# Second layers two first layers later, gate rounding on GpSimd, and a third tile's copies on VectorE, in a fused attention and MLP kernel

## The chip, the cores and the metric

The kernel runs on one core of a Trainium2 chip. Its engines work side by side, each through its own queue in order: TensorE (PE in the profile; PEld are its weight loads), VectorE (DVE), ScalarE (ACT), GpSimd (POOL) and SyncE (SP, which issues most DMAs). The metric is the device time of one execution in microseconds (us), as a median of several runs.

## The reference

Banded attention (each query sees the last 96 keys and 8 global ones, with a slope per head), and then a two-layer MLP over its output. All in float32.

```python
scores = scale * np.matmul(q, k.transpose(0, 1, 3, 2))      # 4 batches, 8 heads, 768 x 768, head size 64
bias = -slopes[:, None, None] * dist[None, :, :]
scores = np.where(keep, scores + bias[None], -1000000000.0)
a = np.exp(scores - np.max(scores, axis=-1, keepdims=True))
a = a / (np.sum(a, axis=-1, keepdims=True) + 1e-09)
x = np.matmul(a, v)                                          # -> 3072 tokens of 512
...
h = x @ w_in                                                 # 512 -> 2048
g = h * np.clip(h + 3.0, 0.0, 6.0) / 6.0
return (g @ w_out).astype(np.float32)                        # 2048 -> 512
```

## The kernel before

**Tiling.** The 3072 tokens are 8 blocks of 384 (three tiles of 128). A block's attention is done in four pairs of heads. A block's MLP runs over 16 slices of 128 hidden columns. For one slice the *first layer* (`first`, L179) is 12 matmuls into one PSUM bank hp (there are two), the *gate* makes g from hp (ACT relu L190, DVE L191), splits it into a rounded part gh (`high`, L197 on GpSimd or L199 on ACT) and the rest gl (`rest`, DVE L204), and the *second layer* (`second`, L211) is 9 matmuls that add gh and gl times w_out into three PSUM banks acc. Each product uses high and low parts, hence the three matmuls where one would do. g has one buffer, gh and gl three each (`common`, L116 and L117).

**Weights.** They lie in memory as 16 words of 1 MB, two 32-bit halves per number, and are decoded on the chip (`decode`, L403). Even words hold two slices of w_in, odd words the same two slices of w_out, so the first layer of slice f needs word f//2*2 and its second layer word f//2*2+1. A word's decoding takes three steps, written here as a, b and c:

- a: the fetch of the word two later, DVE L417 and L418, ACT L395
- b: DVE L424 of the word before (its low part)
- c: DVE L427 (needs L395 and L418), then for the next word ACT L384 and GpSimd L388, then ACT L431 (the high part)

The scratch `we`, which L388 writes, L395 completes and L427 reads, has one buffer; L388 of the next word therefore follows L427 of this one.

**Stages.** (1) The attention of blocks 0 and 1: eight pairs, each as scores (L862), `weigh` (DVE L877, ACT L881), normalizing (GpSimd L901), `turn` (PE transposes of each of the three tiles, L909 and L911, and the copy pt of them from PSUM, L913), and `values` (L953) with `put_x` (ACT L165 for xh, DVE L166 for xl). In it `self.more` is true until the last scores are out: up to then (pairs 0 to 5) tile 1's copy runs on DVE, those of tiles 0 and 2 on ACT; afterwards all on ACT. (2) The MLP of block 0, with four slices of block 1 among it, while the weights are still being decoded; it begins in the last two pairs' `turn`. (3) The other 12 slices of block 1 beside the attention of block 2 (`beside`, L630). (4) Blocks 2 to 7, each beside the attention of the next.

**What sets the order.** The instructions of PE, SyncE and GpSimd run in the order of the program (`in_order`, L651). Those of DVE and ACT are put in order by the framework's scheduler, at build time. The program order of stage 2 comes from the generator `halves` (L452): for each slice of `order` (L619) it emits the first layer and the gate, then the second layer of the slice before, kept in `self.last`, and yields after each. `work` (L434) keeps two counters, one for PE time and one for DVE time, and emits a decoding step whenever DVE's is behind; `decoded_to` (L447) forces the steps that the next layer needs. `finish` (L488) emits the pending second layer.

`order` puts slices 0 to 3 of block 1 behind slices 4, 7, 10 and 13 of block 0. `halves` is called without `pool` for blocks 0 and 1, so that gh is rounded on ACT (L199), and with it from block 2 on (L197).

Of the kernel before, what the change touches and what calls it, by code (L numbers as in the profile page):

```python
# [26 lines left out]
NF = DF // P  # L27
# [23 lines left out]
BESIDE = 12  # L51
LEAST_AHEAD = 4
WORDS = 2
# [9 lines left out]
class Kernel:  # L63
# [377 lines left out]
    def decode_step(self):  # L441
        self.given[1] += next(self.decoding_steps)
        self.decoded += 1
        if self.decoded == 3 * (NF + 1):
            self.decoded_all()

    def decoded_to(self, i):  # L447

        while self.decoded < 3 * (i + 1) + (2 if i < NF - 1 else 3):
            self.decode_step()  # L450

    def halves(self, steps, pool=False):  # L452


        for block, f, x, acc in steps:
            self.decoded_to(f // 2 * 2)
            g = self.gate(self.first(f, x), block == len(self.blocks) - 1 and f == NF - 1)
            gh = self.high(g, pool) if pool else None
            self.work(2.1, 0.47)
            yield  # L460
            if not pool:
                gh = self.high(g, pool)
            gl = self.rest(g, gh)
            self.work(0, 0.47)
            if self.last is not None:
                self.finish()
                yield
            self.last = (block, f, acc, gh, gl)

# [18 lines left out]
    def finish(self):  # L488
        block, f, acc, gh, gl = self.last
        self.decoded_to(f // 2 * 2 + 1)  # L490
        self.second(f, acc, gh, gl)
        if f == NF - 1 and block < len(self.blocks) - 1:
            b, tb = self.blocks[block]
            self.store(b * S + tb * TB, acc)
        self.ended = block, f
        self.work(2.1, 0)
        self.last = None

    def banded(self, flag):
# [9 lines left out]
        self.raw, self.z, self.e, self.given, self.decoded = {}, {}, {}, [0.0, 0.0], 0  # L509
        self.last, self.op, self.ended = None, None, None  # L510
        self.weights()
        with ExitStack() as early, ExitStack() as words:
# [69 lines left out]
            self.weights()  # L582
            self.allowed = 3 * (NF + 1)
            acc1 += [pool.tile([P, BANK], F32, name=name) for pool, name in ((self.ps_s, "sp"), (self.ps_t, "tp"), (self.ps_x, "xp"))]
# [14 lines left out]
        for i in range(2, len(self.blocks)):  # L599
            units, x_next = [], None  # L600
            if i + 1 < len(self.blocks):
                x_next = self.x_tiles()
                units, ahead = self.attention(i + 1, x_next, ahead)
                if i == 2:
                    units = [[]] + units
            else:
                units = [[]] * 4 + [[lambda: self.doubt(flag)]]
            acc = self.acc_tiles()
            steps = [(i, f, x, acc) for f in range(NF)]
            for k, _ in enumerate(self.halves(steps if x_next else steps[:-3], True)):  # L610
                for unit in units[k] if k < len(units) else ():
                    unit()
            if not x_next:
                self.end(steps[-3:])
            x = x_next
# [3 lines left out]
    def order(self, xs, acc, acc1):  # L619
# [3 lines left out]
        for f in range(NF):  # L623
            steps.append((0, f, xs[0], acc))
            while done * (NF - LEAST_AHEAD) < (f + 1 - LEAST_AHEAD) * (NF - BESIDE):
                steps.append((1, done, xs[1], acc1))
                done += 1
# [171 lines left out]
class Pair:  # L799
# [103 lines left out]
    def turn(self, t):  # L903
# [8 lines left out]
        c = slice(0, 1 if lo else 2)  # L912
        (nc.vector.tensor_copy if kk.more and t == 1 else nc.scalar.copy)(out=pt[:, :, c], in_=tp[:, :, c])  # L913
        self.pts.append(pt)
# [120 lines left out]
```

## Time and profile before

| | us |
|---|---|
| median of 3 runs (lowest to highest) | 677.55 (677.43 to 677.74) |
| the profiled execution | 679.32 |
| its span, first to last instruction | 677.5 |

The profile is of one execution, whose time is 1.8 us over its span. Three views of it are read below: the page (share of each engine), the waits (which engine waited for whom), and windows and timelines (busy time of each engine in a stretch, and its instructions one by one: start in us, duration in us, engine, line, operation, what is written and read, and in brackets the idle time before it and what ended it). A duration on the timeline can overlap the next instruction's, so a queue's pace is read from the starts.

The 40 slices of the page, each 16.9 us long, in tenths of busy time, and the clock that TensorE was granted:

```profile
PE   9878898999998999999999999999999999999997
DVE  6778899524564776557662677547763677422222
ACT  6988899434553444143332444143331433221111
PEclk9969899999999999999999999999999999999999
```

Stages 1 and 2 fill the first nine slices, to about 152 us; stage 3 ends near 214 us.

### The profile page before, as it was taken

The page shows a single profiled execution, that of the slowest core. Times are in us where ns is not written, and L with a number is a line of the kernel's source. Part 1 is how long each engine was busy: PE and PEld are TensorE (multiplying, and loading weights), DVE is VectorE, ACT ScalarE, POOL GpSimd, SP SyncE. Part 2 cuts the span into 40 slices and gives each one's busy share as a digit, 9 for nine tenths or more (in the row PEclk, how much of TensorE's full clock was granted, in tenths as well). Part 3 has the DMA queues.
Part 4 walks back from the last instruction along what each step waited for, and adds up shares of the span by engine and source line. Part 5 has one row for each costly group of instructions (what it writes and reads, how often), then busy time and mean ns, then how long its engine had stood idle before and what let it go on. Part 6 is the DMA issues. An engine that isn't in the chain of part 4 may idle for free.

```text
span 677.5 us, 11187 instructions
## 1 busy us (share of the span) xinstructions
PE 655.5 (97%) x3923; PEld 582.1 (86%) x3923; DVE 406.7 (60%) x1068; ACT 294.3 (43%) x714; POOL 212.3 (31%) x373
## 2 busy tenths in 40 slices
PE   9878898999998999999999999999999999999997
PEld 7667787898787999999998999899998999999995
DVE  6778899524564776557662677547763677422222
ACT  6988899434553444143332444143331433221111
POOL 5744232001221333325340444404541344302110
PEclk9969899999999999999999999999999999999999
DMA  8645655003575357634554257634455155500001
GB/s 321 185 162 180 247 218 186 1 1 97 153 210 156 98 156 194 171 105 125 153 157 126 91 148 194 172 112 117 125 164 156 62 154 150 139 33 18 1 1 51
DMA packets 67169, 89.56 MB, mean 132 GB/s; under 512 B 10656, under 2 KB 53920, under 8 KB 65056
## 3 DMA queue, kind: packets, MB, share of 16 engines
q1 hardware_dynamic: 66816, 88.49, 43.8%
q8 instruction: 33, 0.54, 0.3%
q14 instruction: 32, 0.26, 0.1%
q10 hardware_dynamic: 288, 0.26, 0.1%
HBM read 65.14 MB, written 23.59 MB: 131 GB/s over the span
## 4 chain that ended last, share of the span: by engine, by line
PE 75%; DVE 9%; DMA 5%; issue 4%; ACT 4%; POOL 2%; SPq 0%; POOLq 0%; DVEq 0%; ACTq 0%
PE hp L179 33%; PE acc L211 31%; PE xp L953 3%; PE sp L866 2%; ACT n L881 2%; DMA load<-pairs 2%; DVE wz L427 2%; PE tp L953 2%; PE tp L866 2%; POOL n L901 1%; DVE n L877 1%; DVE wz L417 1%; DMA wst<-w 1%; DVE g L191 1%; DVE gl L204 1%
## 5 line engine op out<-in xcount | busy, mean ns | idle before, releaser
L190 ACT ACTIVATE g<-hp,small 128x384 f32<-128x384 f32 x127 | 73.6, 580 | 246.0 <-PE hp L179 228.5
L179 PE MATMUL hp<-xh,w1h 128*128 128x384 f32 x512 | 174.6, 341 | 0.0
L179 PE MATMUL hp<-xh,w1l 128*128 128x384 f32 x512 | 172.9, 338 | 0.0
L179 PE MATMUL hp<-xl,w1h 128*128 128x384 f32 x512 | 172.5, 337 | 0.0
L197 POOL TENSOR_SCALAR gh<-g 128x384 fp32r<-128x384 f32 x96 | 51.8, 540 | 296.6 <-DVE g L191 257.5
L211 PE MATMUL acc<-w2h,gl 128*128 128x512 f32 x336 | 133.7, 398 | 5.4 <-DVE gl L204 5.4
L901 POOL TENSOR_SCALAR n<-n,sums 128x232 f32<-128x232 f32 (+1 forms) x186 | 99.0, 548 | 108.6 <-ACT n L881 61.1
L211 PE MATMUL acc<-w2h,gh 128*128 128x512 f32 x336 | 132.4, 394 | 0.4 <-ACT gh L199 0.4
L211 PE MATMUL acc<-w2l,gh 128*128 128x512 f32 x336 | 132.3, 394 | 0.0
L191 DVE SCALAR_TENSOR_TENSOR g<-g,hp 128x384 f32<-128x384 f32 x128 | 69.8, 545 | 89.8 <-ACT g L190 89.4
L881 ACT ACTIVATE n<-n,least 128x232 f32<-128x232 f32 (+1 forms) x192 | 89.2, 466 | 50.5 <-DVE least L877 49.8
L204 DVE TENSOR_TENSOR gl<-g,gh 128x384 fp32r<-128x384 f32 x128 | 78.4, 613 | 52.5 <-POOL gh L197 44.9
L179 PEld LDWEIGHTS hp<-xh,w1h 128*128 128x128 f32 x512 | 96.7, 189 | 6.0 <-issue 2.2
L179 PEld LDWEIGHTS hp<-xl,w1h 128*128 128x128 f32 x512 | 96.7, 189 | 3.7
L179 PEld LDWEIGHTS hp<-xh,w1l 128*128 128x128 f32 x512 | 96.5, 188 | 0.0
L211 PEld LDWEIGHTS acc<-w2h,gl 128*128 128x128 f32 x336 | 63.1, 188 | 23.0 <-DVE gl L204 9.5
L926 DVE STREAM_TRANSPOSE blocks<-n 128x256 f32<-128x256 f32 x132 | 51.5, 425 | 36.3 <-POOL n L901 25.4
L211 PEld LDWEIGHTS acc<-w2h,gh 128*128 128x128 f32 x336 | 63.3, 188 | 10.7 <-ACT gh L199 0.7
L211 PEld LDWEIGHTS acc<-w2l,gh 128*128 128x128 f32 x336 | 63.2, 188 | 10.1
L877 DVE CUSTOM_DVE_ANT_0 n<-sp,d 128x232 f32<-128x232 f32 (+1 forms) x70 | 23.7, 376 | 30.8 <-PE sp L866 30.5
L388 POOL TENSOR_SCALAR we<-wst 128x1024 int32<-128x1024 uint32 x16 | 22.7, 1416 | 46.1 <-DVE wz L427 37.5
L881 ACT ACTIVATION_READ_ACCUMULATOR n<-n,least 128x1 f32 x192 | 36.1, 188 | 0.0
(120 smaller groups left out, 745.6 us busy)
## 6 DMA issues: line engine op xcount, KB each, us to landing
wst<-w SPq DMA_DIRECT2D x16, 1024.0 KB, 4.9
there<-blocks SPq DMA_DIRECT2D x60, 256.0 KB, 2.6
load<-pairs SPq DMA_DIRECT2D x20, 636.0 KB, 5.2
load<-pairs SPq DMA_DIRECT2D x32, 384.0 KB, 4.1
weights<-there SPq DMA_DIRECT2D x48, 192.0 KB, 4.0
weights<-there SPq DMA_DIRECT2D x48, 160.0 KB, 3.2
out<-o SPq DMA_DIRECT2D x23, 256.0 KB, 2.0
load<-pairs SPq DMA_DIRECT2D x11, 444.0 KB, 4.4
```

The lines of the kernel that those rows point to most:

```text
L179: self.nc.tensor.matmul(hp, lhsT=self.w1(w, f)[:, kt, :], rhs=a[:, kt, :], start=(n == 0), stop=(n == 3 * NKT - 1))
L190: nc.scalar.activation(out=g, in_=hp, func=AF.Relu, bias=self.three, scale=1.0)
L191: nc.vector.scalar_tensor_tensor(out=g, in0=g, scalar=6.0, in1=hp, op0=ALU.min, op1=ALU.mult)
L197: self.nc.gpsimd.tensor_scalar(out=gh, in0=g, scalar1=1.0, scalar2=0.0, op0=ALU.mult, op1=ALU.add)
L204: self.nc.vector.tensor_tensor(out=gl, in0=g, in1=gh.bitcast(F32), op=ALU.subtract)
L211: self.nc.tensor.matmul(acc[tt], lhsT=a[:, tk], rhs=self.w2(w, f), start=(f == 0 and j == 0), stop=(f == NF - 1 and j == 2))
L866: nc.tensor.matmul(sp[j][:, lo:W], lhsT=q[:, t], rhs=part["kx"][:, c], start=(m == 0), stop=(m == 1))
L877: nc.vector.tensor_tensor_reduce(out=e[:, j, lo:W], in0=sp[j][:, lo:W], in1=d, op0=ALU.add, op1=ALU.min, scale=scale, scalar=3.0e38, accum ...
L881: nc.scalar.activation(out=e[:, j, lo:W], in_=e[:, j, lo:W], func=AF.Exp, bias=self.least[:, i:i + 1], scale=-1.0, accum_out=self.sums[:, ...
L901: nc.gpsimd.tensor_scalar(out=e[:, j, lo:W], in0=e[:, j, lo:W], scalar1=over, scalar2=0.0, op0=ALU.mult, op1=ALU.add)
L926: nc.vector.transpose(out=blocks[:, :, s].rearrange("p b j q -> p j b q"), in_=e[:, :, c:c + P].rearrange("p j (b q) -> p j b q", b=4))
L953: nc.tensor.matmul(xps[j * D:(j + 1) * D, t * P:(t + 1) * P], lhsT=vt[0:K, t, j * D:(j + 1) * D], rhs=self.part(t, j, c, K), start=(c == 0 ...
```

## The change

- While the weights are being decoded, `self.last` is a list of up to two pending second layers: that of a slice is emitted after the first layer of the slice two later in the list. Once all is decoded, it is one again.
- Before a first layer whose word is not yet decoded, the pending second layers are emitted.
- `order` puts the four slices of block 1 behind slices 3, 4, 5 and 6 of block 0.
- gh is rounded on ACT only in slices started before the end of stage 1 (`self.early`, cleared there); the other slices of blocks 0 and 1 use GpSimd.
- While `self.more` holds, DVE copies tile 2's transposes as well as tile 1's.

With the first layer of block b, slice f written Fb.f and the second Sb.f, the program order of PE's halves from the last pairs on, worked out from the two counters, is:

```
before: F0.0 F0.1 S0.0 F0.2 S0.1 F0.3 S0.2 F0.4 S0.3 F1.0 S0.4 F0.5 S1.0 F0.6 S0.5 F0.7 S0.6 F1.1 S0.7 F0.8 S1.1 F0.9 S0.8 F0.10 S0.9 F1.2 S0.10 F0.11 S1.2 F0.12 S0.11 F0.13 S0.12 F1.3 S0.13 F0.14 S1.3 F0.15 S0.14 F1.4 S0.15
after:  F0.0 F0.1 S0.0 S0.1 F0.2 F0.3 F1.0 S0.2 F0.4 S0.3 F1.1 S1.0 F0.5 S0.4 F1.2 S1.1 F0.6 S0.5 F1.3 S1.2 F0.7 S0.6 F0.8 S1.3 F0.9 S0.7 F0.10 S0.8 F0.11 S0.9 F0.12 S0.10 S0.11 F0.13 S0.12 F0.14 S0.13 F0.15 S0.14 F1.4 S0.15
```

```diff
-LEAST_AHEAD = 4
+LAG = 3
...
-        if self.decoded == 3 * (NF + 1):
+        if self.decoded == self.all_steps:
             self.decoded_all()
 
+    def ready(self, i):
+        return self.decoded >= 3 * (i + 1) + (2 if i < NF - 1 else 3)
+
     def decoded_to(self, i):
-        while self.decoded < 3 * (i + 1) + (2 if i < NF - 1 else 3):
+        while not self.ready(i):
             self.decode_step()
 
-    def halves(self, steps, pool=False):
+    def halves(self, steps):
         for block, f, x, acc in steps:
+            while self.last and not self.ready(f // 2 * 2):
+                self.finish()
+                yield
             self.decoded_to(f // 2 * 2)
             g = self.gate(self.first(f, x), block == len(self.blocks) - 1 and f == NF - 1)
+            pool = not self.early
             gh = self.high(g, pool) if pool else None
             self.work(2.1, 0.47)
             yield
...
             gl = self.rest(g, gh)
             self.work(0, 0.47)
-            if self.last is not None:
+            while len(self.last) >= (2 if self.decoded < self.all_steps else 1):
                 self.finish()
                 yield
-            self.last = (block, f, acc, gh, gl)
+            self.last.append((block, f, acc, gh, gl))
...
     def finish(self):
-        block, f, acc, gh, gl = self.last
+        block, f, acc, gh, gl = self.last.pop(0)
...
             self.weights()
-            self.allowed = 3 * (NF + 1)
+            self.early = False
+            self.allowed = self.all_steps
...
             steps.append((0, f, xs[0], acc))
-            while done * (NF - LEAST_AHEAD) < (f + 1 - LEAST_AHEAD) * (NF - BESIDE):
+            if LAG <= f < LAG + NF - BESIDE:
                 steps.append((1, done, xs[1], acc1))
                 done += 1
...
-        (nc.vector.tensor_copy if kk.more and t == 1 else nc.scalar.copy)(out=pt[:, :, c], in_=tp[:, :, c])
+        (nc.vector.tensor_copy if kk.more and t > 0 else nc.scalar.copy)(out=pt[:, :, c], in_=tp[:, :, c])
```

More of the change, by code (lines that the diff above doesn't have):

```diff
@@ L496, in finish @@
         self.work(2.1, 0)
-        self.last = None
     def banded(self, flag):
@@ L509, in banded @@
         self.raw, self.z, self.e, self.given, self.decoded = {}, {}, {}, [0.0, 0.0], 0
-        self.last, self.op, self.ended = None, None, None
+        self.last, self.op, self.ended, self.early, self.all_steps = [], None, None, True, 3 * (NF + 1)
         self.weights()
@@ L609, in banded @@
             steps = [(i, f, x, acc) for f in range(NF)]
-            for k, _ in enumerate(self.halves(steps if x_next else steps[:-3], True)):
+            for k, _ in enumerate(self.halves(steps if x_next else steps[:-3])):
                 for unit in units[k] if k < len(units) else ():
```

## The prediction

> **What bounds the kernel now.** I read the page first, then what TensorE (PE) waits for, then its stretches. A *half* below is one first layer (12 matmuls, L179) or one second layer (9 matmuls, L211) of one slice; F0.3 is the first layer of block 0, slice 3, and S1.0 the second layer of block 1, slice 0.
>
> ```profile
> span 677.5 us, 11187 instructions
> PE 655.5 (97%) x3923; PEld 582.1 (86%) x3923; DVE 406.7 (60%) x1068; ACT 294.3 (43%) x714; POOL 212.3 (31%) x373
> L197 POOL TENSOR_SCALAR gh<-g 128x384 fp32r<-128x384 f32 x96 | 51.8, 540 | 296.6 <-DVE g L191 257.5
> ...
> PE acc L211 <- DVE gl L204: 5.4, 8, 1.9
> PE xp L953 <- issue: 5.2, 2, 3.2
> PE acc L953 <- DMA weights<-there: 2.4, 2, 2.2
> ```
>
> PE is busy nearly throughout, and its listed waits are small: 5.4 us of second layers waiting for gl (the gate's rest, made by VectorE, DVE), 5.2 us in the early attention, 2.4 us for a DMA near 212 us. Matmul ends are modelled, so a slow stretch hides more than the listed gaps. The windows show it: the stretch from F0.3 to the end of block 0, and the undisturbed half of it.
>
> ```profile
> 68.21:120.71 52.50, 47.51 (x224) 40.81 (x223) 50.08 (x62) 48.59 (x53) 16.00 (x11) 0.97 0.55 206
> 127.62:152.53 24.91, 24.91 (x127) 22.67 (x126) 6.72 (x13) 7.24 (x14) 0.00 (x0) 1.00 0.00 1
> ...
> 68.21:152.53 84.32, 41.79 (x216) 39.53 (x217) 0.98 0.35 128
> 127.62:152.53 24.91, 13.51 (x72) 12.71 (x72) 1.00 0.00 1
> ...
> 68.21:152.53 84.32, 42.66 (x162) 29.59 (x162) 0.98 0.35 128
> 127.62:152.53 24.91, 13.35 (x55) 10.05 (x54) 1.00 0.00 1
> ```
>
> (First pair: PE, weight loads, DVE, ACT, POOL, clock; second pair L179 alone; third L211 alone.) Undisturbed, 72/12 + 54/9 = 12 halves take 24.91 us, 2.076 us each. From 68.21 to 152.53 there are 216/12 + 162/9 = 36 halves; at 2.076 they need 74.7 us and took 84.3. **9.6 us are lost**, all before 122 us, where DVE is busy 50.08 of 52.50 us. One round there:
>
> ```profile
> 91.84 0.54 DVE L204 TENSOR_TENSOR gl<-g,gh 128x384 fp32r<-128x384 f32 x1
> 92.31 1.21 DVE L427 CUSTOM_DVE_ANT_0 wz<-wz,we 128x2048 uint16<-128x2048 uint16 x1
> 93.44 0.68 DVE L417 TENSOR_SCALAR wz<-wz 128x1024 f32<-128x1024 f32 x1
> 94.05 0.54 DVE L191 SCALAR_TENSOR_TENSOR g<-g,hp 128x384 f32<-128x384 f32 x1
> 94.51 1.17 DVE L418 TENSOR_SCALAR wz<-wz 128x1024 int32<-128x1024 int32 x1
> 95.60 1.21 DVE L424 TENSOR_TENSOR w2l<-wz,w2h 128x1024 fp32r<-128x1024 f32 x1
> 96.73 0.55 DVE L204 TENSOR_TENSOR gl<-g,gh 128x384 fp32r<-128x384 f32 x1
> ...
> 92.43 0.50 PE L211 MATMUL acc<-w2h,gl 128*128 128x512 f32 x1 [0.39 <-DVE gl L204]
> ...
> 93.60 1.53 POOL L388 TENSOR_SCALAR we<-wst 128x1024 int32<-128x1024 uint32 x1 [3.36 <-DVE wz L427]
> ...
> 94.62 0.52 ACT L199 CAST gh<-g 128x384 fp32r<-128x384 f32 x1
> 95.16 1.47 ACT L395 ACTIVATE we<-wst,small 128x1024 f16<-128x1024 int32 x1
> ```
>
> DVE repeats every 4.89 us (91.84 to 96.73): one word decoded (3.95 us by the starts) and one gate (0.94). PE needs 2 x 2.076 = 4.15 us for the slice, then its second layer meets a gl that lies behind L418 and L424. The loss is a queue order, not missing weights: the L424 at 95.60 is the tenth (word 9), while PE at that time runs slice 6, whose second layer needs word 7.
>
> **The change part by part.** *Lag of two.* S of a slice now follows F of the slice two later in the list, so a gate has four halves (8.3 us) instead of two (4.15). In the round above a first layer ended near 91.5 (its second-layer neighbour already waits at 92.43) and its gl at 97.2: 5.7 us, covered. Nothing else of PE's work changes, so the most to be had is **-9.6**. If DVE falls behind, the cover is gone; that is the term after next.
>
> *The order near the attention's end.* With no word ready for F0.2, pending second layers now go first: S0.1 stands before F0.2.
>
> ```profile
> 62.44 0.42 PE L179 MATMUL hp<-xh,w1h 128*128 128x384 f32 x1
> ...
> 64.60 0.39 PE L211 MATMUL acc<-w2h,gh 128*128 128x512 f32 x1
> ...
> 62.54 0.50 ACT L199 CAST gh<-g 128x384 fp32r<-128x384 f32 x1
> ...
> 63.93 0.55 DVE L204 TENSOR_TENSOR gl<-g,gh 128x384 fp32r<-128x384 f32 x1
> ```
>
> Before, F0.2 (62.44) covered the gate of slice 1, and S0.1 started at 64.60. Now S0.1 can start two matmuls at about 63 and waits for gl until 64.4; it ends at 66.1 instead of PE having done two halves by 66.74 with F0.2 still to do. F0.3 moves from 68.2 to 69.7: **+1.5** (0 if gl comes earlier in DVE's queue, 2.1 at most, a whole half).
>
> *GpSimd rounding.* L199 ran on ACT 32 times; the first four slices keep it, 28 gh move to POOL at 0.54 instead of 0.51 us. ACT's relief is worth nothing by itself, as PE waits for DVE. But POOL's order is that of the program, and working the two counters through by hand gives, from F0.4 on: gh of the sixth slice, L388 of word 6, gh of the seventh (F1.1), L388 of word 7, and so on to gh of the fifteenth (F0.10), L388 of word 15. Gate and word are now in lockstep. So word 7's L388 waits for F1.1, five halves after 69.7: 80.1, done 82.2, its gh at about 84.2. Then one round per word, c long. The sixteenth gl (F0.11) follows L388 of word 15: 84.2 + 8c + 1.53 + 0.54 + 0.47 + 0.2 of handing over. PE wants it for S0.11, 27 halves after 69.7: 125.75. With c = 4.89 it comes at 126.05, 0.3 late. What is late next is this gate, not a weight: word 14 would be finished some 6 us before F0.14.
>
> c itself grows if POOL and DVE disturb each other:
>
> ```profile
> 69.41 1.12 POOL L388 TENSOR_SCALAR we<-wst 128x1024 int32<-128x1024 uint32 x1 [8.23 <-DMA wst<-w]
> ...
> 71.54 0.68 DVE L418 TENSOR_SCALAR wz<-wz 128x1024 int32<-128x1024 int32 x1
> ```
>
> L418 takes 0.68 us alone and 1.17 beside L388; L388 takes 1.12 alone and 1.53 beside L417. One more POOL instruction per round costs DVE from 0 to another 0.49. I take c = 5.05, a third of that, since gh (0.54) is a third of L388: gl at 127.3, **+1.6** (0.3 with c = 4.89, 4.2 with 5.38). The Trainium skill, SBUF — State Buffer, section "Who interferes with whom", says that the two engines share one port pair under an exclusive lock, and that a DVE instruction with two SBUF inputs also contends with GpSimd's reads. By that rule gh also has to get past L424 and gl, and the sum would be nearer that of the first rival; the two L418 rows agree that one blocks the other.
>
> *The clock.* A wait of PE can be followed by half clock:
>
> ```profile
> 77.75 0.50 PE L211 MATMUL acc<-w2h,gl 128*128 128x512 f32 x1 [1.89 <-DVE gl L204]
> ...
> 80.00:82.00 2.00, 2.00 (x8) 2.00 (x7) 2.00 (x2) 1.90 (x2) 0.46 (x1) 0.50 0.18 66
> ...
> 210.00:212.00 2.00, 0.39 (x2) 0.00 (x0) 0.56 (x1) 0.06 (x1) 0.00 (x0) 1.00 0.97 243
> 214.00:216.00 2.00, 2.00 (x12) 2.00 (x13) 0.56 (x1) 0.43 (x1) 0.00 (x0) 1.00 0.47 101
> ```
>
> After the 1.89 us wait the granted clock was 0.50; after the 2.2 us wait near 212 us it stayed 1.00. The new wait before S0.1 is about 1 us; a spell of half clock costs 0 to 1.4 us. I take **+0.5**. The Trainium skill, TensorE: Matmul & The Clock Gate, section "HAM oscillation — how this bites in real kernels", puts the danger at gaps over some 3.4 us; the 1.89 us row does not agree. By the Trainium skill's figure this term would be 0 and the sum -6.5.
>
> *The third tile's copies.* Six L913 copies move from ACT to DVE:
>
> ```profile
> L913 DVE COPY pt<-hp x6: 679/681/691, 15.7 to 44.3; 128x512 f32<-128x512 f32 x6
> L913 ACT COPY pt<-hp x6: 569/587/593, 18.6 to 48.2; 128x512 f32<-128x512 f32 x6
> ...
> 31.47 0.17 DVE L891 TENSOR_SCALAR sums<-sums 128x6 f32<-128x6 f32 x1 [1.07 <-ACT n L881]
> ...
> 35.39 0.48 PE L953 MATMUL xp<-pt,load 128*64 128x128 f32 x2 [3.15 <-issue]
> ```
>
> ACT saves 6 x 0.587 = 3.5 us, DVE gains 6 x 0.68 = 4.1. DVE idles about 1 us per pair just where the copy would fall (1.07 before L891). But if it lands ahead of xl (L166), for which the values matmuls wait (the 3.15 us gap), PE loses it. Bounds -3.5 and +4.1; nearest to the idle row, I take **+0.4**.
>
> *Beside the attention of block 2.* ACT's gh lay between two exponentials of the last pair:
>
> ```profile
> 201.11 0.50 ACT L199 CAST gh<-g 128x384 fp32r<-128x384 f32 x1
> 201.51 0.49 ACT L881 ACTIVATE n<-n,least 128x232 f32<-128x232 f32 x1
> ```
>
> That chain ends in the 2.2 us wait, so it shortens by 0.4: **-0.4** (0 if POOL's queue takes it back). The other gh there are hidden: from the first layer to gl is some 2.5 us of 4.15. Loads and fetches keep their places in SyncE's order.
>
> **Sum:** -9.6 + 1.5 + 1.6 + 0.5 + 0.4 - 0.4 = -6.0. The profiled execution took 679.3 us around its 677.5 us span, 1.8 over the median of 677.55; the sum is a difference, so span 671.5, and median **671.5**.
>
> **The rivals.**
> 1. *The port.* c = 5.38: -9.6 + 1.5 + 4.2 + 0.5 + 0.4 - 0.4 = -3.4, **674.1**. For it: L418's two rows. Against: POOL idles 3.36 us per round, so gh can fall beside instructions that it doesn't disturb. The section of the Trainium skill's SBUF — State Buffer named above is the rule beside it.
> 2. *The round turns into a loop (slower).* Place: DVE's queue from word 7 to 15. If g (L191) stays behind L427 and L417, as in the round shown, then L388 must wait for gh, gh for g, g for L427, and L427 for L395 and L388. Price: 1.13 + 0.61 + 0.46 + 0.54 + 1.53 + 1.47 + about 0.3 of handing over = 6.0 us per round; the sixteenth gl comes at 134.9, 9.2 late: +1.6, **679.2**. It decides from c = 5.80 on, where the delay (7.6) uses up the rest of the sum. For: the order shown. Against: g is now earlier in the program than that L427, and PE, running ahead, has it ready.
> 3. *It doesn't do what it says.* DVE is busy 95% of the stretch; if words, not gl, hold PE as soon as it runs faster, waits only change their name: **677.5**. Against: words are ahead of PE by two at 95.60.
> 4. *ACT's relief shortens the attention* as well (-3.5 instead of +0.4): **667.6**. Against: the removed copies often stood in ACT's idle time.
>
> **Chances.** Forecast 0.51 (669 to 673.5), port 0.13, attention 0.10, no change 0.10, slower loop 0.16. Faster by over 0.2% (1.4 us, about what a measurement here can tell from none): 0.51 + 0.13 + 0.10 = 0.74; within 0.10; slower 0.16. The range reaches from just under the attention case to just over the loop: 667.0 to 680.0; what it leaves out are two terms at their far ends together.
>
> **What would show it.** Right: no PE wait for gl after 70 us; 36 halves from F0.3 in about 77 us; a wait before S0.1 near 63 us; L388 in step with gh, rounds of about 5 us. Port: L418 or L424 longer than 1.2 us. Loop: L427, g, gh, L388 in a chain, rounds near 6 us, PE waiting for gl near 120 us. Wrong altogether: the attention's values matmuls waiting longer than 3.15 and 2.0 us for xl, or F0.3 later than 70 us.

## The result and the profile after

| | before | after |
|---|---|---|
| median, same chip (lowest to highest), us | 677.64 (677.43 to 680.10) | 685.75 (684.42 to 686.95) |
| after / before, with 95% interval | | 1.0111 [1.0081, 1.0141] |
| profiled execution and its span, us | 679.3, 677.5 | 685.4, 683.6 |

The change makes the kernel slower by 1.1%, 7.5 us of 677.6; the forecast was 671.5, 667 to 680. The head of the page after and its row for gh on GpSimd (L197), and then what PE waited for longest (in all, times, longest, in us; L960 is L953 of the kernel before):

```profile
span 683.6 us, 11207 instructions
...
PE 652.8 (95%) x3923; PEld 579.4 (85%) x3923; DVE 417.1 (61%) x1074; ACT 279.0 (41%) x680; POOL 235.6 (34%) x401
...
L197 POOL TENSOR_SCALAR gh<-g 128x384 fp32r<-128x384 f32 x124 | 73.9, 596 | 378.9 <-DVE g L191 343.2
```

```profile
PE hp L179 <- DVE g L191: 8.4, 6, 1.6
PE xp L960 <- issue: 3.6, 2, 2.3
PE acc L211 <- POOL gh L197: 3.1, 1, 3.1
PE acc L211 <- DVE gl L204: 2.7, 2, 1.6
```

PE waits less for gl than before (2.7 instead of 5.4 us), and 8.4 us for g instead, which sets a bank hp free, and 3.1 us for gh. The change does what it says: there are 28 more L197, and their mean is 596 ns instead of 540.

**Where the time went.** From the start of S0.15, the last second layer of block 0, to the end of the span it is 527.0 us before and 527.6 after; all else lies ahead of it. What sets that start can be read from two things: when VectorE begins the last decoding step of word 15 (the last L424), and how many halves PE has left by then. The starts of both in the timelines of VectorE and PE, before:

```profile
123.97 1.23 DVE L424 TENSOR_TENSOR w2l<-wz,w2h 128x1024 fp32r<-128x1024 f32 x1 [0.65 <-ACT w2h L431]
...
150.46 0.39 PE L211 MATMUL acc<-w2h,gh 128*128 128x512 f32 x1
```

and after:

```profile
138.51 1.23 DVE L424 TENSOR_TENSOR w2l<-wz,w2h 128x1024 fp32r<-128x1024 f32 x1
...
156.01 0.39 PE L211 MATMUL acc<-w2h,gh 128*128 128x512 f32 x1
```

Word 15 comes 14.5 us later: 5.7 us of it are there already at the L424 of word 6 (86.67 us after, 80.93 before), whose L388 now stands behind a gate in GpSimd's order, and the rest comes in the rounds behind it. S0.15 comes 5.5 us later, since PE does more of its halves in the longer decoding: counted by matmuls (12 to a first layer, 9 to a second), 12.75 are left before S0.15 at 123.97 before, 7.8 at 138.51 after. 12.75 x 2.076 = 26.5 us, which is what the two rows of before lie apart. After, 7.8 x 2.076 = 16.2 of 17.5 us; the granted clock was 0.50 from 138 to 140 us, behind a wait of 3.05 us (shown below), and that is most of the rest. This sum is used for every kernel below: **S0.15 starts at word 15 plus 2.076 us for each half left.** It holds within 0.3 us for all of them but after (1.3 us more) and f3 (2.6 us more, where PE waited 1.94 us behind word 15 and then had half clock too).

**The round after.** VectorE's timeline in the stretch, one round:

```profile
102.59 1.60 DVE L417 TENSOR_SCALAR wz<-wz 128x1024 f32<-128x1024 f32 x1
104.23 0.69 DVE L418 TENSOR_SCALAR wz<-wz 128x1024 int32<-128x1024 int32 x1
104.84 1.22 DVE L424 TENSOR_TENSOR w2l<-wz,w2h 128x1024 fp32r<-128x1024 f32 x1
105.97 0.55 DVE L191 SCALAR_TENSOR_TENSOR g<-g,hp 128x384 f32<-128x384 f32 x1
106.44 1.22 DVE L427 CUSTOM_DVE_ANT_0 wz<-wz,we 128x2048 uint16<-128x2048 uint16 x1
108.07 0.56 DVE L204 TENSOR_TENSOR gl<-g,gh 128x384 fp32r<-128x384 f32 x1 [0.41 <-POOL gh L197]
108.55 1.59 DVE L417 TENSOR_SCALAR wz<-wz 128x1024 f32<-128x1024 f32 x1
```

and GpSimd's, with the row of PE in which the wait for gh ends behind it in a fence of its own:

```profile
102.16 1.48 POOL L388 TENSOR_SCALAR we<-wst 128x1024 int32<-128x1024 uint32 x1
106.67 1.36 POOL L197 TENSOR_SCALAR gh<-g 128x384 fp32r<-128x384 f32 x1 [3.03 <-DVE g L191]
108.12 1.48 POOL L388 TENSOR_SCALAR we<-wst 128x1024 int32<-128x1024 uint32 x1
```

```profile
137.82 0.80 PE L211 MATMUL acc<-w2h,gh 128*128 128x512 f32 x1 [3.05 <-POOL gh L197]
```

The round (102.59 to 108.55) is 5.95 us, against 4.89 before, and the two engines take turns: gh, ready with g at 106.5, is drawn out to 1.36 us while L427 runs (540 ns was its mean before); gl waits 0.41 us for it; then L388 runs, and L417 beside it takes 1.60 instead of 0.68. L418, drawn out before (1.17), is now short (0.69). By the starts, L417 takes 1.03 us more than alone (1.64 instead of 0.61) and the wait for gh 0.50, and L418 gives back 0.48: together the 1.05 us by which the round grew. The wait of PE at 137.82 is the sixteenth gate, F0.11's, which the prediction's third term and its second rival were about.

### The profile page after: what moved, and what is told of

It reads as the page before. It is cut to its first block, busy times and chain, and to the rows that moved or that the text cites. A ratio compares the mean times of both kernels' runs of the same rounds, so it can differ in the third digit from the quotient of the medians.

```text
span 683.6 us, 11207 instructions
## 1 busy us (share of the span) xinstructions
PE 652.8 (95%) x3923; PEld 579.4 (85%) x3923; DVE 417.1 (61%) x1074; ACT 279.0 (41%) x680; POOL 235.6 (34%) x401
## 4 chain that ended last, share of the span: by engine, by line
PE 78%; DVE 6%; POOL 5%; DMA 4%; ACT 3%; issue 2%; SPq 0%; POOLq 0%; DVEq 0%; ACTq 0%
PE hp L179 35%; PE acc L211 32%; POOL n L908 2%; ACT n L888 2%; PE xp L960 2%; PE sp L873 2%; PE tp L960 2%; DVE wz L417 2%; PE tp L873 2%; POOL gh L197 1%; DMA load<-pairs 1%; DMA wst<-w 1%; DVE g L191 1%; DVE wz L418 1%; PE sp L211 1%
## 5 line engine op out<-in xcount | busy, mean ns | idle before, releaser
L197 POOL TENSOR_SCALAR gh<-g 128x384 fp32r<-128x384 f32 x124 | 73.9, 596 | 378.9 <-DVE g L191 343.2
L179 PE MATMUL hp<-xh,w1h 128*128 128x384 f32 x512 | 175.0, 342 | 8.4 <-DVE g L191 8.4
L179 PE MATMUL hp<-xh,w1l 128*128 128x384 f32 x512 | 172.9, 338 | 0.0
L179 PE MATMUL hp<-xl,w1h 128*128 128x384 f32 x512 | 172.3, 336 | 0.0
L211 PE MATMUL acc<-w2h,gh 128*128 128x512 f32 x336 | 133.6, 398 | 4.8 <-POOL gh L197 3.1
L211 PE MATMUL acc<-w2h,gl 128*128 128x512 f32 x336 | 133.5, 397 | 2.7 <-DVE gl L204 2.7
L211 PE MATMUL acc<-w2l,gh 128*128 128x512 f32 x336 | 132.8, 395 | 0.0
L191 DVE SCALAR_TENSOR_TENSOR g<-g,hp 128x384 f32<-128x384 f32 x128 | 69.8, 546 | 88.9 <-ACT g L190 88.4
L908 POOL TENSOR_SCALAR n<-n,sums 128x232 f32<-128x232 f32 (+1 forms) x186 | 100.4, 556 | 40.6 <-DVE sums L899 25.3
L179 PEld LDWEIGHTS hp<-xh,w1h 128*128 128x128 f32 x512 | 96.7, 189 | 16.7 <-DVE g L191 10.9
L179 PEld LDWEIGHTS hp<-xl,w1h 128*128 128x128 f32 x512 | 96.6, 189 | 3.5
L179 PEld LDWEIGHTS hp<-xh,w1l 128*128 128x128 f32 x512 | 96.3, 188 | 0.0
L211 PEld LDWEIGHTS acc<-w2h,gl 128*128 128x128 f32 x336 | 63.5, 189 | 18.0 <-DVE gl L204 4.2
L211 PEld LDWEIGHTS acc<-w2h,gh 128*128 128x128 f32 x336 | 63.6, 189 | 16.1 <-POOL gh L197 3.8
L211 PEld LDWEIGHTS acc<-w2l,gh 128*128 128x128 f32 x336 | 63.8, 190 | 10.1
L836 POOL TENSOR_SCALAR kx<-load 64x504 fp32r<-64x504 f32 (+1 forms) x40 | 31.3, 782 | 1.6
```

The lines of the kernel that those rows point to most:

```text
L179: self.nc.tensor.matmul(hp, lhsT=self.w1(w, f)[:, kt, :], rhs=a[:, kt, :], start=(n == 0), stop=(n == 3 * NKT - 1))
L191: nc.vector.scalar_tensor_tensor(out=g, in0=g, scalar=6.0, in1=hp, op0=ALU.min, op1=ALU.mult)
L197: self.nc.gpsimd.tensor_scalar(out=gh, in0=g, scalar1=1.0, scalar2=0.0, op0=ALU.mult, op1=ALU.add)
L211: self.nc.tensor.matmul(acc[tt], lhsT=a[:, tk], rhs=self.w2(w, f), start=(f == 0 and j == 0), stop=(f == NF - 1 and j == 2))
L836: nc.gpsimd.tensor_scalar(out=part["kx"][own, c], in0=k[own, c], scalar1=1.0, scalar2=0.0, op0=ALU.mult, op1=ALU.add)
L908: nc.gpsimd.tensor_scalar(out=e[:, j, lo:W], in0=e[:, j, lo:W], scalar1=over, scalar2=0.0, op0=ALU.mult, op1=ALU.add)
```

## The experiments

The theory after the result: the two GpSimd instructions of a round hold VectorE up, and each other, through a common port; VectorE is the pace of the stretch, and PE's waits for gl only show it. Its rivals: the lag itself, or the early slices, bring the loss by a new queue order; or the loss is one of order near the attention's end. All runs with their numbers (us; *round*: spacing of the L424; *w15*: start of the last L424; *left*: halves left then, S0.15 not counted; ratio to before on the same chip):

| run | is | median | before | ratio [95%] | round | w15 | left | S0.15 |
|---|---|---|---|---|---|---|---|---|
| before | | 677.64 | | | 4.89 | 124.0 | 12.75 | 150.5 |
| after | | 685.75 | 677.64 | 1.0111 [1.0081, 1.0141] | 5.95 | 138.5 | 7.8 | 156.0 |
| e1_act | after, gh on ACT | 680.65 | 679.53 | 1.0014 [0.9996, 1.0032] | 5.34 | 125.2 | 12.9 | 152.1 |
| e2_lag1 | after, lag one | 684.86 | 679.53 | 1.0063 [1.0036, 1.0089] | 5.95 | 138.8 | 7.7 | 154.9 |
| e3_copy | before + copies | 676.00 | 679.53 | 0.9929 [0.9904, 0.9954] | 4.89 | 120.9 | 12.75 | 147.3 |
| e4_pool | before + gh on GpSimd | 685.28 | 679.53 | 1.0069 [1.0045, 1.0093] | 5.94 | 140.3 | 7.7 | 156.5 |
| e5_side | before + unrelated GpSimd work | 680.31 | 680.13 | 1.0010 [0.9993, 1.0028] | 5.11 | 124.3 | 12.75 | 150.8 |
| e6_tiny | e1 + one-column read | 677.65 | 680.13 | 0.9971 [0.9952, 0.9990] | 5.34 | 133.9 | 7.4 | 149.7 |
| e7_bdve | before, L388 on VectorE | 680.85 | 680.13 | 1.0018 [0.9999, 1.0037] | 5.01 | 123.9 | 12.75 | 150.4 |
| e8_first | e1, F0.2 first | 676.08 | 680.13 | 0.9943 [0.9923, 0.9963] | 5.34 | 124.7 | 10.9 | 147.4 |
| f1_nolag | e8, lag one | 676.38 | 679.62 | 0.9951 [0.9932, 0.9970] | 4.89 | 120.7 | 12.75 | 147.1 |
| f2_lag | e8, old slice places | 679.42 | 679.62 | 0.9998 [0.9979, 1.0017] | 5.34 | 123.0 | 12.9 | 149.9 |
| f3_tiny | e8 + one-column read | 687.40 | 679.62 | 1.0104 [1.0063, 1.0146] | 6.53 | 140.3 | 8.0 | 159.5 |
| f4_dve | e8, L388 on VectorE | 672.11 | 679.62 | 0.9882 [0.9841, 0.9923] | 5.01 | 121.3 | 11.0 | 144.0 |
| g1_round | f4, gh on GpSimd | 673.82 | 679.53 | 0.9924 [0.9906, 0.9943] | 5.32 | 126.1 | 9.5 | 145.8 |
| g2_nolag | f4, lag one | 677.34 | 679.53 | 0.9967 [0.9953, 0.9980] | 5.01 | 121.1 | 12.75 | 147.6 |
| g3_dve | f4 again | 673.21 | 679.53 | 0.9902 [0.9885, 0.9919] | 5.01 | 121.1 | 10.9 | 143.8 |

The kernel before had medians from 677.64 to 680.13 on the chips used, so ratios are compared below, not times from different rows. A ratio is taken over all runs of both kernels and can differ from the quotient of the two medians, by 0.2% at most here.

### One part of the change at a time

**e1_act**: after, with gh rounded on ACT until all is decoded.

```diff
-            pool = not self.early
+            pool = self.decoded == self.all_steps
```

> The changed kernel with one thing undone: while the weights are being decoded, gh is rounded by ScalarE again (GpSimd takes over when the decoding is done). Port theory (in the changed kernel GpSimd's rounding waits for VectorE's L427 and GpSimd's L388 then holds up VectorE's L417, which makes each round 5.95 us): the rounds fall to about 4.9 us, TensorE runs at full speed from the fourth first layer on, 36 halves in 75 to 77 us from 68.5 us, median 668 to 671. Rival, order theory (the loss comes from the lag and the four early slices, which let the words fall behind the gates): rounds stay above 5.5 us and the median at 680 or more.

**e2_lag1**: after, with a lag of one.

```diff
-            while len(self.last) >= (2 if self.decoded < self.all_steps else 1):
+            while len(self.last) >= 1:
```

> The changed kernel without the lag: at most one second layer pending, GpSimd still rounds. Port theory: rounds of 5.9 us as in the changed kernel, and now the second layers wait for gl as well, median 685 to 690. Order theory: without the lag the words keep pace, rounds near 4.9 us, median 677 to 680.

**e3_copy**: before, with the third tile's copies on VectorE alone.

```diff
-        (nc.vector.tensor_copy if kk.more and t == 1 else nc.scalar.copy)(out=pt[:, :, c], in_=tp[:, :, c])
+        (nc.vector.tensor_copy if kk.more and t > 0 else nc.scalar.copy)(out=pt[:, :, c], in_=tp[:, :, c])
```

> The kernel before with one part of the change alone: VectorE copies the third tile's transposes too. Both theories leave the rounds at 4.89 us. If the copies shorten the attention (the first of the MLP's first layers started at 43.2 us in the changed kernel against 48.4 before), it starts about 5 us earlier here, and the median is 673 to 675; if a later wait (the weights' DMA) takes that back, 676 to 678.

**e4_pool**: before, with gh on GpSimd from the end of stage 1 on, alone.

```diff
-    def halves(self, steps, pool=False):
+    def halves(self, steps):
...
+            pool = not self.early
...
+            self.early = False
```

> The kernel before with one part of the change alone: after the attention GpSimd rounds the gates of blocks 0 and 1. No lag, slices in the old places, copies as before. Port theory: rounds of 5.9 us instead of 4.89 for some ten words, median 684 to 690. Order theory: rounds of 4.9 us, median 677 to 679.

Measured: e4 shows that GpSimd's rounding is the loss by itself: 1.0069, rounds of 5.94 us, without lag, early slices or copies. e1 takes it out of the whole change: 1.0014 instead of 1.0111. The copies alone gain 0.7% (e3), where the forecast had a small loss. The lag makes no gain inside the change: with it the ratio is 1.0111, without it 1.0063, and the intervals just overlap, so it may cost some 3 us there.

But e1 missed what I expected: its rounds fell only to 5.34 us, not to about 4.9, and it stayed at the time of before. VectorE's timeline of e1_act shows a round without any GpSimd gh in it:

```profile
101.51 1.21 DVE L427 CUSTOM_DVE_ANT_0 wz<-wz,we 128x2048 uint16<-128x2048 uint16 x1
102.64 0.68 DVE L417 TENSOR_SCALAR wz<-wz 128x1024 f32<-128x1024 f32 x1
103.25 1.48 DVE L204 TENSOR_TENSOR gl<-g,gh 128x384 fp32r<-128x384 f32 x1
104.65 0.68 DVE L418 TENSOR_SCALAR wz<-wz 128x1024 int32<-128x1024 int32 x1
...
106.85 1.21 DVE L427 CUSTOM_DVE_ANT_0 wz<-wz,we 128x2048 uint16<-128x2048 uint16 x1
```

GpSimd's timeline of the same kernel has the L388 that lies beside it:

```profile
102.81 1.51 POOL L388 TENSOR_SCALAR we<-wst 128x1024 int32<-128x1024 uint32 x1 [3.83 <-DVE wz L427]
```

With the lag, gh is ready early, and the framework puts gl right behind L417, beside L388, where it takes 1.48 us instead of 0.55; without lag gl stands behind L424, and only L418 (0.48 us longer) lies beside L388. So the lag has a price of its own, 0.45 us a round. There is still one gate to each word, and VectorE has no idle time.

### What one more instruction costs in the round

**e5_side**: before, with a GpSimd multiplication by one of an unrelated 128x280 tile after each slice's first layer while decoding.

```diff
+        self.side = self.const.tile([P, 280], F32, name="side")
+        self.nc.vector.memset(self.side, 1.0)
...
+            if self.allowed == 3 * (NF + 1) and self.decoded < self.allowed:
+                self.nc.gpsimd.tensor_scalar(out=self.side, in0=self.side, scalar1=1.0, scalar2=0.0, op0=ALU.mult, op1=ALU.add)
```

> The kernel before with one idle instruction more: in each slice that starts between the end of the attention and the end of the decoding, GpSimd also multiplies an unrelated tile of 128x280 by one, in the place where the changed kernel rounds. Nothing waits for it, and VectorE's order is that of before. Port theory (GpSimd and VectorE block each other while one of them holds the way to SBUF): L418, which already stands beside L388, is held up 0.3 to 0.4 us longer, rounds of 5.2 to 5.3 us instead of 4.89, and the median 2.5 to 4 us over the kernel before. Dependency theory (GpSimd costs something only because gates and words wait for each other in its queue): rounds of 4.89 us and the time of before.

**e6_tiny**: e1_act, with a GpSimd read of one column of g ahead of the next L388, so that L388 waits for the gate as in after, while hardly anything is computed.

```diff
+        self.side = self.const.tile([P, 1], F32, name="side")
...
+            if not self.early and not pool:
+                self.nc.gpsimd.tensor_scalar(out=self.side, in0=g[:, 0:1], scalar1=1.0, scalar2=0.0, op0=ALU.mult, op1=ALU.add)
```

> The run e1_act (ScalarE rounds while decoding) plus the dependency alone: GpSimd reads one column of g (128x1) in the place where the changed kernel rounds, so that L388 of a word still waits for the gate in front of it. Port theory: the tiny instruction holds nothing up, rounds of 5.3 us as in e1_act, median within 1 us of it. Dependency theory: rounds of 5.9 us as in the changed kernel, median 5 us over the kernel before.

**e7_bdve**: before, with L388 on VectorE, so that GpSimd has nothing in the round.

```diff
-        self.nc.gpsimd.tensor_scalar(out=self.e[i], in0=words[:, :, 0].bitcast(U32), scalar1=2.0 ** -29, scalar2=0.0, op0=ALU.mult, op1=ALU.add)
+        self.nc.vector.tensor_scalar(out=self.e[i], in0=words[:, :, 0].bitcast(U32), scalar1=2.0 ** -29, scalar2=0.0, op0=ALU.mult, op1=ALU.add)
```

> The kernel before with L388 on VectorE, so that GpSimd does nothing while the weights are decoded after the attention. Port theory: L418 takes 0.68 us instead of 1.16 in every round, and a round is 4.41 us plus what L388 takes on VectorE (0.6 to 1.2): 5.0 to 5.6. Dependency theory, or L418 slow for a reason of its own: L418 stays at 1.16, rounds of 5.5 to 6.1 us. Median 1 to 8 us over the kernel before, by the round.

**e8_first**: e1_act, with the early end of pending second layers left out ahead of F0.2, which so goes ahead of S0.0 and S0.1 (a lag of two from there on).

```diff
-            while self.last and not self.ready(f // 2 * 2):
+            while self.last and not self.ready(f // 2 * 2) and f != 2:
...
-            pool = not self.early
+            pool = self.decoded == self.all_steps
```

> The run e1_act with F0.2 in front of S0.1 again, as in the kernel before. If the swap costs what the changed kernel's profile shows there (waits of 1.7 us before S0.1 and a slow first layer behind it), F0.3 starts at 64 to 66 us instead of 67.3 and the median is 1.5 to 3 us under e1_act. If the rounds of VectorE set the pace from there on anyway, it is within 1 us of e1_act.

Measured: the unrelated work in e5 took 0.75 us and lengthened the round by 0.22 (the instruction of L424 took 1.44 instead of 1.21), near the 0.16 that the prediction had taken for gh; VectorE's order stayed that of before. The median did not rise by the 2.5 us or more that I expected: at 1.0010 it can't be told from before. gh itself lengthens the round by 1.05 (e4). So it isn't one more GpSimd instruction as such, but where it lies. e6 shows one there:

```profile
105.08 1.10 POOL L468 TENSOR_SCALAR side<-g 128x1 f32<-128x1 f32 x1 [2.70 <-DVE g L191]
```

VectorE's L427 (L428 in that kernel) runs from 104.91 for 1.22 us; the read of a single column took 1.10 us and ended at 106.18, just behind it. It is L427 that holds GpSimd there, although GpSimd has hardly anything to do. e6 surprised me otherwise: its word 15 comes 8.7 us later than e1's, and it is faster (0.9971 against 1.0014), since VectorE takes three gates more ahead of word 6's L427 (four, where e1 takes one there and the others later). PE so has 5.5 halves fewer left. After has the same four gates there and the same late word 6 (86.7 us in both), so this delay is not its loss; the longer round is. A gate costs VectorE 0.94 us, and once taken frees PE to do 4.15 us of work beside the decoding.

e7 shows L388 at 0.70 us on VectorE, and L418 back from 1.17 to 0.70: the round grows by 0.12 only. VectorE had been paying 0.48 of the 0.6 us already, as a wait.

e8 gives 0.9943 where e1 gives 1.0014: the rule "pending second layers first" at F0.2 costs 0.7%, 4.8 us, from the same rounds, more than the 1.5 to 3 us that I expected. The windows from word 15 to S0.15 show how (PE busy and matmuls, weight loads, clock); first e1_act, L179 and L211:

```profile
125.20:152.06 26.86, 13.48 (x73) 12.68 (x72) 1.00 0.01 1
...
125.20:152.06 26.86, 15.32 (x64) 11.74 (x65) 1.00 0.01 1
```

and e8_first:

```profile
124.69:147.41 22.72, 11.23 (x61) 10.57 (x60) 1.00 0.00 1
...
124.69:147.41 22.72, 13.11 (x54) 10.06 (x55) 1.00 0.00 1
```

One first layer (12 rows) and one second layer (10 rows, one of them at the window's edge) fewer are left: one whole slice, whose busy time is 2.25 + 2.21 us, and 4.14 us (26.86 - 22.72) of the window; that makes up most of the 4.65 us by which S0.15 is earlier. F0.2 starts at 52.6 among the last transposes in e8, at 63.6 in e1.

### Lag and places, from a kernel without the two losses

**f1_nolag** is e8 with `len(self.last) >= 1`; **f2_lag** is e8 with the four slices of block 1 back in the places of before; **f3_tiny** is e8 with e6's one-column read; **f4_dve** is e8 with L388 on VectorE after stage 1.

```diff
-            while len(self.last) >= (2 if self.decoded < self.all_steps else 1):
+            while len(self.last) >= 1:
```

> The run e8_first (ScalarE rounds while decoding, F0.2 in front of S0.1) without the lag: one second layer pending at most; the copies and the four early slices stay. Pace theory (VectorE, which does one gate and one word per round, sets the pace, and the lag only changes where TensorE waits): the rounds are 4.89 us as in the kernel before, since L388 then stands beside L418 again and not beside gl (5.34 in e8_first), and the median is 1 to 4 us under e8_first. Lag theory (TensorE gains by the lag, and e8_first lost that gain only to its longer rounds): 2 us or more over e8_first, with waits for gl in each round.

```diff
-            if LAG <= f < LAG + NF - BESIDE:
+            while done * (NF - 4) < (f + 1 - 4) * (NF - BESIDE):
```

> The run e8_first with the four slices of block 1 in the places of before (behind slices 4, 7, 10 and 13) and the lag kept. Pace theory: 5.34 us rounds, within 2 us of e8_first. If the four early slices matter (gates done before the words hold TensorE), 2 us or more over it.

```diff
+            if not self.early and not pool:
+                self.nc.gpsimd.tensor_scalar(out=self.side, in0=g[:, 0:1], scalar1=1.0, scalar2=0.0, op0=ALU.mult, op1=ALU.add)
```

> The run e6_tiny (GpSimd reads one column of g in front of L388) with F0.2 in front of S0.1. Here VectorE's queue takes two gates more before word 6, and its round has before's order. Pace theory: a gate more ahead of the words costs VectorE 0.94 us before the decoding ends and saves TensorE 4.15 us after it, rounds about 4.9 us: 2 to 4 us under e8_first. Otherwise the time of e8_first within 1 us.

```diff
-        self.nc.gpsimd.tensor_scalar(out=self.e[i], in0=words[:, :, 0].bitcast(U32), scalar1=2.0 ** -29, scalar2=0.0, op0=ALU.mult, op1=ALU.add)
+        (self.nc.gpsimd if self.early else self.nc.vector).tensor_scalar(out=self.e[i], in0=words[:, :, 0].bitcast(U32), scalar1=2.0 ** -29, scalar2=0.0, op0=ALU.mult, op1=ALU.add)
```

> The run e8_first with L388 on VectorE once the attention of blocks 0 and 1 is emitted, so that GpSimd does nothing beside the rounds. Port theory: gl takes 0.55 us instead of 1.47, rounds of 5.0 us (4.41 and 0.60) instead of 5.34, median 2 to 4 us under e8_first. If gl is slow beside L417 for another reason, rounds of 5.9 us, and 4 us over it.

Measured: f1 ties with e8. The lag leaves one slice fewer (10.9 instead of 12.75 halves, 3.9 us) and makes the eight rounds before word 15 0.45 us longer (3.6 us): it pays back what it takes. With the old places (f2) 12.9 halves are left: the lag then puts nothing ahead, and its rounds are still long; the early places are worth 0.55%, 3.7 us, with the lag. But f2 doesn't show the places alone: in PE's timeline of f2 the 27 matmuls of S0.1, S0.2 and S0.3 follow one another from 64.3 to 72.2 us, since the rule "pending second layers first" empties the list in front of F0.4, which has no slice of block 1 ahead of it in that order; it is what happens at F0.2 in e1. The places without that rule were not tried.

f3 missed, and by much: I expected it faster than e8, since e6 was faster than e1. Its rounds are 6.53 us. VectorE's and GpSimd's timelines of f3_tiny:

```profile
98.82 1.23 DVE L428 CUSTOM_DVE_ANT_0 wz<-wz,we 128x2048 uint16<-128x2048 uint16 x1 [1.12 <-ACT we L396]
...
100.56 0.55 DVE L191 SCALAR_TENSOR_TENSOR g<-g,hp 128x384 f32<-128x384 f32 x1
...
105.34 1.23 DVE L428 CUSTOM_DVE_ANT_0 wz<-wz,we 128x2048 uint16<-128x2048 uint16 x1 [1.12 <-ACT we L396]
```

```profile
101.27 0.50 POOL L468 TENSOR_SCALAR side<-g 128x1 f32<-128x1 f32 x1 [3.97 <-DVE g L191]
101.85 1.97 POOL L389 TENSOR_SCALAR we<-wst 128x1024 int32<-128x1024 uint32 x1
```

Here g stands behind L427 and L417 in VectorE's queue (L428 and L418 in that kernel), the read waits for g, L388 for the read, L395 for L388 and the next L427 for L395, with VectorE idle for 1.12 us of each round. In e6 and in after g stands ahead of L427. This is the loop of the prediction's second rival, with the one-column read in the place of gh. e6 has the same read and doesn't close it, since the framework gave g another place there.

f4 takes GpSimd out of the round, so that gl has nothing beside it: 0.9882, the fastest here, with the lag's slice kept and rounds of 5.01.

### What was still open

Whether gh on GpSimd costs anything once L388 is gone from there, and whether the lag gains where its order costs nothing. **g1_round** is f4 with gh on GpSimd again, **g2_nolag** f4 with a lag of one, **g3_dve** f4 once more.

```diff
-            pool = self.decoded == self.all_steps
+            pool = not self.early
```

> The run f4_dve (L388 on VectorE after the attention) with the rounding on GpSimd again, as in the changed kernel: GpSimd then has one instruction per round instead of two. If the changed kernel's 5.95 us come from the two GpSimd instructions together (gh waits for L427, L388 then holds up L417), one alone costs VectorE at most its own 0.5 us: rounds of 5.0 to 5.5 us, 0 to 4 us over f4_dve. If rounding on GpSimd is slow in itself, rounds of 5.9 us and 7 us or more over f4_dve.

```diff
-            while len(self.last) >= (2 if self.decoded < self.all_steps else 1):
+            while len(self.last) >= 1:
```

> The run f4_dve without the lag: one second layer pending at most. Rounds of 5.0 us in both, since VectorE's queue has the same six instructions and L388. Pace theory: within 1.5 us of f4_dve. Lag theory: 2 us or more over it, with waits for gl in each round.

> The run f4_dve again, on the same chip as the two others, to compare them with: 1.0 to 1.4% under the kernel before.

Measured: gh alone on GpSimd adds 0.31 us to the round (5.32 instead of 5.01) and some 0.2% (0.9924 against 0.9902, intervals that overlap a little); its row in GpSimd's timeline and that of L418 beside it in VectorE's, of g1_round:

```profile
104.41 0.79 POOL L197 TENSOR_SCALAR gh<-g 128x384 fp32r<-128x384 f32 x1 [4.53 <-DVE g L191]
```

```profile
104.75 1.00 DVE L418 TENSOR_SCALAR wz<-wz 128x1024 int32<-128x1024 int32 x1
```

So gh on GpSimd lengthens the round by 0.31 us where L388 is on VectorE, and by 1.05 where it shares GpSimd with L388. That it is a second instruction isn't enough: e5's, with the same L388, cost 0.22.

At equal rounds the lag gains 0.65% (g3 0.9902, g2 0.9967), 4.4 us. PE's waits between 60 and 130 us, g2_nolag:

```profile
PE acc L211 <- DVE gl L204: 3.9, 6, 1.0
PE sp L211 <- DVE gl L204: 3.2, 4, 1.4
```

and g3_dve:

```profile
PE hp L179 <- DVE g L191: 4.8, 8, 0.6
```

The waits for gl are gone with the lag, as the prediction wanted, and 4.8 us of waiting for g stand in their place. Word 15 comes at 121.1 in both. What the lag gains is again the slice that PE has done before the rounds begin (10.9 instead of 12.75 halves left, 3.9 us), not the waits in them.

## Why the prediction was wrong

**Lag, -9.6: the step that failed first.** "The loss is a queue order, not missing weights" took PE's waits for gl as what could be had. They were slack. In the rounds VectorE had no idle time and gave one gate to each word, and so PE could do one slice (4.15 us of work) in a round of 4.89, however its halves were ordered. The row that said so stood in the prediction: 50.08 busy of 52.50 us. Measured, the lag is worth 4.4 us where rounds are equal (g2, g3), nothing where the new order puts gl beside L388 (f1 against e8), and no gain in the changed kernel (e2). The third rival, that waits only change their name, had the mechanism right for the rounds.

**GpSimd rounding, +1.6: the mechanism right, the size not.** The prediction had the chain that came true: GpSimd's order in step with the gates, the sixteenth gate late for S0.11. Word 7's L388 ran at 85.64 (84.2 forecast); the eight rounds from there took 46.3 us to word 15's L388 at 131.91 (40.4 forecast, c = 5.05); and the gate's way from there to S0.11 took 5.9 us (2.74 forecast), as its g stood behind L417, L418 and L424. That makes 137.82 instead of 127.3. c was 5.95, beyond the first rival's 5.38 and past the 5.80 from which the second decides. The cause is the first rival's, that the two engines hold each other up, but in both directions and with two GpSimd instructions in a round: gh behind L427, L417 behind L388. The price by runs is 4.7 us (e4 against before, 0.69%) to 6.6 (after against e1, 1.0111 - 1.0014).

**The second rival** had the sign, the place and, by luck, the round (6.0 us for 5.95; gl at 134.9 and 679.2 us were still too early and too low), by a chain that was not the one: in after g stood ahead of L427, as the prediction's "against" said. It does exist, in f3. The forecast of 0.16 for it came from asking only whether that one chain closes; 5.8 us a round could be passed in another way, and was.

**S0.1 ahead of F0.2, +1.5, and the clock, +0.5: near what was counted, and counted against the wrong thing.** With copies in both, F0.3 starts at 67.3 in e1 and 66.4 in e3, 0.9 us later, inside the bounds of 0 and 2.1. In after the waits and the half clock were there, and the clock cost more than the term: some 3.4 us at 0.50 from 62.6 to 66 us lose about 1.7 us, beyond the bound of 1.4 for which the prediction shows no row, and a second spell, from 138 us on, followed the wait for gh. PE's rows of after with the idle time in brackets, and two windows of it (the clock is the number before the last two):

```profile
59.81 0.50 PE L211 MATMUL acc<-w2h,gh 128*128 128x512 f32 x1 [0.65 <-ACT gh L199]
61.58 0.50 PE L211 MATMUL acc<-w2h,gl 128*128 128x512 f32 x1 [1.04 <-DVE gl L204]
```

```profile
62.00:64.00 2.00, 2.00 (x8) 1.58 (x7) 1.23 (x1) 0.14 (x1) 0.00 (x0) 0.65 0.98 384
64.00:66.00 2.00, 2.00 (x8) 2.00 (x7) 0.00 (x0) 0.24 (x1) 0.18 (x1) 0.50 1.02 430
```

What was missed is that the rule also takes back the lag at F0.2: ended early, the two second layers cost the one slice that the lag would have put ahead. 4.8 us (e1 against e8), and with it all that the lag had to give.

**The third tile's copies, +0.4: wrong sign.** They gain 0.71% [0.46, 0.96], 4.8 us (e3; its two medians are 3.5 us apart), at the bound of -3.5 or just beyond, and the fourth rival (ACT's relief shortens the attention) had the sign and the place right. From word 6 on, words come 3.1 us earlier (word 15 at 120.9 instead of 124.0). The argument against that rival, that ACT's removed copies often stood in its idle time, was no ground for a term of nearly nothing: VectorE, ACT and GpSimd are all busier in the window below in e3, since the same work is done sooner. The windows of 36 to 52 us (PE, weight loads, VectorE, ACT, GpSimd, clock), before:

```profile
36.00:52.00 16.00, 14.00 (x106) 11.84 (x104) 10.16 (x29) 12.98 (x33) 7.49 (x11) 0.72 0.60 200
```

e3_copy, and e5_side, which has the attention of before:

```profile
36.00:52.00 16.00, 12.51 (x103) 10.98 (x102) 14.89 (x33) 14.93 (x32) 12.24 (x15) 0.89 0.79 269
```

```profile
36.00:52.00 16.00, 11.33 (x117) 9.41 (x113) 11.98 (x33) 14.49 (x36) 9.84 (x13) 1.00 0.68 218
```

In before's profiled execution PE ran a part of this stretch at half clock, and F0.0 started at 48.4; in e5 it did not, with the same attention, and F0.0 started at 45.2; in e3 at 43.8. The L424 of word 5, ahead of the rounds, came at 76.0 in before, 74.0 in e5 and 72.9 in e3. So some 2 of the 3.1 us between these two profiles are the clock of one execution, and 1.1 are left. (Word 15 of e5 can't be used for this, as its rounds are longer.) The clock is not all that e3 gains: on its chip the one execution of before with a granted clock of 1.000 took 677.85 us, and e3's six, with 0.993 to 0.996, have a median of 676.00. How the gain is divided between a shorter attention and a clock that is halved for less time, and which of the copies' waits went, was not tried.

**Beside block 2's attention, -0.4:** nothing of it is seen, and nothing can be: from S0.15 to the end it is 0.6 us longer, but that stretch varies from 526.0 to 529.5 us in the profiles of all these kernels. **Sum:** the medians' 7.5 us go by ratios into -4.8 for the copies (e3), +0.9 for lag and early places together (e8 against e3), +4.8 for the second layers ahead of F0.2 (e1 against e8) and +6.6 for GpSimd's rounding (after against e1). Each has an uncertainty of about 2 us, and each holds for the order in which the parts are put together here.

**The signs set out beforehand.** "L388 in step with gh" came, "36 halves in about 77 us" did not: S0.15 starts 87.5 us after F0.3, for 35 halves. "No PE wait for gl after 70 us" held and showed nothing, since the wait had moved to g, and once to gh. The port's sign was set on L418 and L424, which took 0.69 and 1.22 us in after as they do alone; it was L417 that grew. Of the loop's signs only rounds near 6 us came.

## What to carry to other kernels

Before a wait of the busiest engine is counted as time to be had, look at the engine that ends it: if that one has no idle time either, reordering moves the wait, and only work taken from that engine, or work that it can do before the stretch begins, makes a gain. The gain can be read as: when is the slow engine done, and how much has the fast one left by then. An instruction moved to GpSimd cost here what it disturbed on VectorE and not its own duration, so price such a move by the rows of what lies beside it in the new order, and expect the scheduler to choose another order when a result is ready earlier.

## What the hardware showed that was not expected

- L427, a custom VectorE instruction with two inputs in SBUF, held GpSimd off to its end: gh took 1.36 us beside it, and a read of one column 1.10 us. L388 in turn held gl (1.48 us instead of 0.55), which has two inputs in SBUF; the Trainium skill, SBUF — State Buffer, section "Who interferes with whom", says that a VectorE instruction with two SBUF inputs contends with GpSimd's reads and that the one issued first has the shared ports, and these rows agree. g (L191), with one input in PSUM, was never drawn out: 0.54 to 0.56 us in all rows above.
- The same instruction costs less on the engine that is short of time: L388 took 1.53 us on GpSimd with 0.48 us of VectorE's time lost beside it, and 0.70 us on VectorE, 0.60 by the starts (e7). GpSimd then has nothing left that could lie beside gl or L417, in whatever order.
- The half clock of PE came and went between executions in the same stretch (0.72 in before, 1.00 in e5, from the same attention), and in after it followed waits of 0.65 and 1.04 us, and one of 3.05 us (0.50 from 138 to 140 us), but none of the six waits of 0.60 to 1.56 us for g, one a round (1.00 from 98 to 134 us).
